# q and k of a head pair in one 128-partition tile, their transposes as 64-row pairs beside the score bursts, another order of the opening, and filling spread by what is ready

## The chip, the cores and the metric

The kernel runs on one core of one Trainium2 chip. The metric is device time in microseconds of one execution, lower is better. The engines named below are PE (TensorE matmul; PEld is its weight load), DVE (VectorE), ACT (ScalarE), POOL (GpSimd) and SP (SyncE, which here only issues DMAs).

## The reference

Block-causal attention, whose output is the input of a maxout feed-forward layer:

```python
# q, k, v: (8 batches, 8 heads, 576 tokens, 64) float32
scores = scale * np.matmul(q, k.transpose(0, 1, 3, 2))
mask = (pos[:, None] // 64) >= (pos[None, :] // 64)
attn = softmax(np.where(mask, scores, -1e9))
x = np.matmul(attn, v).transpose(0, 2, 1, 3).reshape(4608, 512)
g = np.maximum(x @ w1, x @ w2)          # w1, w2: (512, 1024)
out = g @ w_out                         # w_out: (1024, 512)
```

## The kernel before

The work goes by head pairs: 8 batches of 4 pairs, p = 0 to 31. The scheduler is switched off, so each engine executes its instructions in the order in which the code writes them, and waits on semaphores where data or a buffer isn't ready.

For one pair p the steps are these. `load_qk` brings q and k (float32) by two DMAs from SP's queue, each with 8 tokens per partition on 72 partitions. `cast_qk` makes bfloat16 of them, on POOL in the steady state. `transposes(p)` does 16 PE transposes (8 of q into `ps_qT`, 8 of k into `ps_kT`), which DVE copies to `qT` and ACT to `kT`. `burst_a` and `burst_b` are the score matmuls: two heads share each step, head 0 on rows 0 to 63 of the PE array and head 1 on rows 64 to 127. They write four PSUM tiles, here u0 and u1 (`burst_a`) and u2 and u3 (`burst_b`), from a pool `ps_s` of two. `exp` on ACT turns each into `aT`, and memsets (`mask`) on POOL clear the lower half of each diagonal block of 128, two after u0 and u1, two after u2. `av(p, [0, 1])` and `av(p, [2, 3, 4])` multiply with v, whose extra column of ones gives the row sums; DVE makes the reciprocal `rec` and the product `xp`. `x_out` transposes `xp` on PE into `ps_x`, and DVE copies that to `xT`.

The feed-forward matmuls are single steps of 512 columns, which a generator gives out: `h_unit` (8 steps, two PSUM tiles, ended by a DVE copy `h` and a DVE maximum into `g`) and `y_unit` (8 steps, ended by an ACT copy and a DMA of the result). `fill(n)` puts up to n of them between the attention steps on PE. A span of 512 tokens may start once `x_out` of the last pair of a batch has raised `done_tokens`. Before, `fill` asks for 11, 5 and 11 steps in each pair and stops when the generator has none. There are 864 steps in all: 64 belong to the first span and 96 to each further one. One span is released by each of the batches 0 to 6 and two by the last batch, and 224 steps are left after pair 31.

All of the PSUM tiles of transposes, av, x_out, h and y share one pool, `ps_m`, of four banks. v, w1, w2 and w_out come by DMAs that POOL issues (they cast on the way), in the same instruction stream as POOL's casts and memsets. In the opening, v's first DMA stands ahead of the memsets that DVE does on the v tiles; w1 and w2 are issued within pair 0, v of batch 1 and w_out within pair 1.

Of the kernel before, what the change touches and what calls it, by code (L numbers as in the profile page):

```python
# [14 lines left out]
def kernel(  # L15
# [68 lines left out]
    def load_qk(p):  # L84
        b, hp = divmod(p, HP)
        raws[p] = []
        for nm, src in (("q", q), ("k", k)):
            t = raw.tile([P, 2, RPP * D], FP32, name=f"{nm}raw")
# [4 lines left out]
            raws[p].append(t)  # L93

    def cast_qk(p, engines):
        qk_n[p] = []
        for nm, t, copy in zip("qk", raws.pop(p), engines):
            n = qkn.tile([P, RPP, 2, D], BF16, name=f"{nm}n")
            copy(  # L99
                out=n[:NP].rearrange("p t h d -> p h t d"),  # L100
                in_=t[:NP].rearrange("p h (t d) -> p h t d", d=D),
            )
            qk_n[p].append(n)
# [89 lines left out]
    def moe():  # L193
        ny = SPAN // P
        for i in range(NSPAN):
            for f in range(NFF):
                while done_tokens[0] < (i + 1) * SPAN:
                    yield False
                for _ in h_unit(i, f):
                    yield True  # L200
# [17 lines left out]
    def transposes(p):  # L218
        b, hp = divmod(p, HP)
        tiles = []  # L220
        for nm, src in zip("qk", qk_n.pop(p)):
            pt = ps_m.tile([P, RPP, NP], BF16, name=f"ps_{nm}T", tag="m")
            for j in range(RPP):
                nc.tensor.transpose(  # L224
                    pt[:, j, :], src[:NP, j].rearrange("p h d -> p (h d)"), ident[:NP, :NP],
                )
            t = (qT_r if nm == "q" else kT_r)[p % NT]
            dst = t[:, :S].rearrange("q (p j) -> q p j", j=RPP)
            sv = pt.rearrange("q j p -> q p j")
            if nm == "q":  # L230
                nc.vector.tensor_copy(out=dst, in_=sv)
            else:
                nc.scalar.copy(out=dst, in_=sv)  # L233
# [16 lines left out]

    def mask(p, a0, n=1, step=0):
        a = aT_r[p % NA]
        if n == 1:
            nc.gpsimd.memset(a[BLK:, :, a0:a0 + BLK], 0.0)  # L254
        else:
            nc.gpsimd.memset(
                a[BLK:, :, a0:a0 + n * step].rearrange("p h (n s) -> p h n s", s=step)[:, :, :, :BLK],
                0.0,
            )

# [11 lines left out]
    def burst_b(p):  # L272
        u2 = ps_s.tile([P, 2, 512], FP32, name="ps_s", tag="s")
        scores(p, u2, 0, 2, 256, 320)
        scores(p, u2, 320, 3, 384, 192)
# [3 lines left out]
        nc.gpsimd.memset(aT_r[p % NA][BLK:, :, 1024:1088], 0.0)  # L279
        nc.gpsimd.memset(aT_r[p % NA][BLK:, :, 1344:1408], 0.0)  # L280
# [41 lines left out]
    for p in range(NPAIR):  # L322
        b, hp = divmod(p, HP)
        burst_a(p)
        fill(11)
        burst_b(p)
        if p + 3 < NPAIR:
            load_qk(p + 3)
        if p + 2 < NPAIR:
# [45 lines left out]
```

## Time and profile before

| | before |
|---|---|
| median of 3 runs | 343.23 us (341.82 to 343.73) |
| profiled execution | 338.89 us, span 337.1 us |
| PE busy | 292.4 us (87%) |
| PE weight loads busy | 157.5 us (47%) |
| DVE busy | 178.5 us (53%) |
| ACT busy | 138.8 us (41%) |
| POOL busy | 125.4 us (37%) |

The span is the time from the first to the last instruction of the profiled execution; the device time holds 1.8 us more. A busy share is an average over stages that differ: here an opening without feed-forward steps, the stage in which attention and filling run together, and a tail of feed-forward steps alone.

### The profile page before, as it was taken

What the parts mean: (1) busy time and instruction counts of PE and PEld (TensorE: products, weight loads), DVE (VectorE), ACT (ScalarE), POOL (GpSimd) and SP (SyncE); (2) the same over time, 40 slices, a digit from 0 to 9 for tenths busy, and PEclk for the clock granted to TensorE, in tenths of its full rate; (3) what the DMA queues carried; (4) which work ended last, traced back from release to release, by engine and by line L of the source; (5) the groups of instructions that cost most, each with busy time, mean ns of one, the idle gap of its engine ahead of it and who ended that gap; (6) DMA issues with size and microseconds to landing.
All of it is one profiled execution on the core that took longest, in us unless ns stands there. A gap on an engine that the chain in (4) does not pass through costs nothing.

```text
span 337.1 us, 7097 instructions
## 1 busy us (share of the span) xinstructions
PE 292.4 (87%) x2880; PEld 157.5 (47%) x2880; DVE 178.5 (53%) x353; ACT 138.8 (41%) x198; POOL 125.4 (37%) x244
## 2 busy tenths in 40 slices
PE   0065469996999999999999999999999998999995
PEld 0053245554555545555555555555555554444442
DVE  0242124775556655665666566656656665455440
ACT  2053434436545454545454545454554444101112
POOL 2329643554554345434543554355433300000000
PEclk9999999999999999999999999999999999999999
DMA  7899997674087559754875478548853000011013
GB/s 144 168 163 185 222 163 173 92 98 26 2 134 110 124 131 135 112 119 133 129 117 120 118 126 121 123 126 111 132 118 98 31 33 34 31 62 64 31 62 124
DMA packets 57984, 36.63 MB, mean 109 GB/s; under 512 B 39008, under 2 KB 44128, under 8 KB 57952
## 3 DMA queue, kind: packets, MB, share of 16 engines
q0 software_dynamic: 42784, 7.87, 31.5%
q1 hardware_dynamic: 15168, 28.32, 29.0%
q8 instruction: 22, 0.36, 0.5%
q14 instruction: 10, 0.08, 0.1%
HBM read 34.60 MB, written 9.44 MB: 131 GB/s over the span
## 4 chain that ended last, share of the span: by engine, by line
PE 80%; DMA 7%; issue 4%; DVE 3%; ACT 2%; POOL 2%; POOLq 0%; ACTq 0%
PE ps_h L165 37%; PE ps_y L183 18%; PE ps_o L295 10%; PE ps_s L241 7%; DMA w_sb<-in_moe_w_dram 4%; DMA vv<-in_v_dram 4%; PE ps_x L314 3%; PE ps_qT L224 2%; PE ps_kT L224 2%; ACT aT L247 2%; DVE xp L303 2%; POOL w_sb L118 1%; DVE rec L301 1%; DVE vv L130 0%; POOL qn L99 0%
## 5 line engine op out<-in xcount | busy, mean ns | idle before, releaser
L247 ACT ACTIVATE aT<-ps_s 128x1024 bf16<-128x1024 f32 (+1 forms) x128 | 99.2, 831 | 120.1 <-PE ps_s L241 119.1
L165 PE MATMUL ps_h<-xT,w_sb 128*128 128x512 bf16 x576 | 139.2, 381 | 0.0
L165 PEld LDWEIGHTS <-w_sb 128*128 128x128 bf16 x576 | 52.3, 98 | 60.7 <-issue 6.2
L172 DVE CAST h<-ps_h 128x512 bf16<-128x512 f32 x72 | 49.6, 689 | 43.9 <-PE ps_h L165 43.5
L183 PE MATMUL ps_y<-wo_sb,g 128*128 128x512 bf16 x288 | 70.6, 379 | 0.0
L174 DVE TENSOR_TENSOR g<-h,ps_h 128x512 bf16<-128x512 bf16 x72 | 49.5, 687 | 13.3 <-PE ps_h L165 12.1
L295 PE MATMUL ps_o<-vv,aT 128*128 128x65 bf16 x960 | 43.6, 200 | 7.8 <-POOL aT L254 6.9
L301 DVE RECIPROCAL rec<-ps_o 128x4 f32<-128x4 f32 x64 | 12.1, 190 | 66.8 <-PE ps_o L295 66.7
L295 PEld LDWEIGHTS <-aT 128*128 128x128 bf16 x960 | 37.8, 102 | 18.9 <-POOL aT L254 7.2
L254 POOL MEMSET aT<- 64x128 bf16 x64 | 12.7, 200 | 85.4 <-ACT aT L247 85.3
L241 PE MATMUL ps_s<-qT,kT 64*128 64x64 bf16 (+4 forms) x384 | 37.0, 296 | 6.2 <-ACT aT L247 5.5
L183 PEld LDWEIGHTS <-g 128*128 128x128 bf16 x288 | 26.9, 98 | 31.1 <-issue 1.3
L189 ACT COPY y<-ps_y 128x512 f32<-128x512 f32 x36 | 21.2, 588 | 48.0 <-PE ps_y L183 42.2
L108 POOL DMA_DIRECT2D vv<-in_v_dram x40 | 33.8, 852 | 11.8 <-DVE vv L129 11.0
L303 DVE TENSOR_TENSOR xp<-ps_o,rec 128x256 bf16<-128x256 f32 x64 | 31.4, 491 | 2.2
L99 POOL CAST qn<-qraw 72x1024 bf16<-72x1024 f32 x30 | 31.2, 1039 | 1.9
L99 POOL CAST kn<-kraw 72x1024 bf16<-72x1024 f32 x30 | 31.3, 1043 | 0.0
L224 PE MATMUL ps_qT<-ident,qn 72*128 72x72 bf16 x256 | 14.8, 205 | 18.0 <-DVE qn L99 18.0
L233 ACT COPY kT<-ps_kT 128x576 bf16<-128x576 bf16 x32 | 20.1, 628 | 22.0 <-PE ps_kT L224 21.9
L241 PEld LDWEIGHTS <-kT 64*128 64x128 bf16 x384 | 14.8, 97 | 30.6 <-issue 22.3
L279 POOL MEMSET aT<- 64x128 bf16 x32 | 6.4, 201 | 55.0 <-ACT aT L247 55.0
L314 PE MATMUL ps_x<-ident,xp 128*128 128x128 bf16 x160 | 17.4, 230 | 8.8 <-DVE xp L303 8.8
(24 smaller groups left out, 109.5 us busy)
## 6 DMA issues: line engine op xcount, KB each, us to landing
qraw<-in_q_dram SPq DMA_DIRECT2D x32, 288.0 KB
kraw<-in_k_dram SPq DMA_DIRECT2D x32, 288.0 KB
out_dram<-y SPq DMA_DIRECT2D x36, 256.0 KB
vv<-in_v_dram POOLq DMA_DIRECT2D x32, 128.0 KB, 5.8
w_sb<-in_moe_w_dram POOLq DMA_DIRECT2D x8, 256.0 KB, 8.1
wo_sb<-in_moe_w_out_dram POOLq DMA_DIRECT2D x2, 512.0 KB, 13.0
vv<-in_v_dram POOLq DMA_DIRECT2D x8, 64.0 KB, 3.3
```

Of the source, the lines that this page charges most:

```text
L99: copy(out=n[:NP].rearrange("p t h d -> p h t d"), in_=t[:NP].rearrange("p h (t d) -> p h t d", d=D),)
L108: nc.gpsimd.dma_start(out=vv[:rows, c, :, :D], in_=v[b, :, c * P:c * P + rows, :].rearrange("h p d -> p h d"),)
L165: nc.tensor.matmul(pt[:], w_sb[:, c, f * P:(f + 1) * P], xT[:, c, t0:t0 + SPAN], start=(c == 0), stop=(c == NDM - 1),)
L172: nc.vector.tensor_copy(out=h1[:], in_=pt[:])
L174: nc.vector.tensor_max(g[:, f, :], h1[:], pt[:])
L183: nc.tensor.matmul(py[:], g[:, f, s * P:(s + 1) * P], wo_sb[:, f, :], start=(f == 0), stop=(f == NFF - 1),)
L224: nc.tensor.transpose(pt[:, j, :], src[:NP, j].rearrange("p h d -> p (h d)"), ident[:NP, :NP],)
L241: nc.tensor.matmul(ps[:m, hh, col:col + w], kT[r, c * P:c * P + m], qT[r, q0:q0 + w], start=True, stop=True,)
L247: nc.scalar.activation(out=aT_r[p % NA][:m, :, a0:a0 + w], in_=ps[:m, :, :w], func=AF.Exp, scale=scale,)
L295: nc.tensor.matmul(po[:, gi, hh, :], a[:, hh, a0:a0 + P], vv[:, c, 2 * hp + hh, :], start=(mm == 0), stop=(mm == n_mm - 1),)
L303: nc.vector.tensor_mul(xp[:, :n], po[:, :, :, :D], rec[:, :n].to_broadcast([P, n, 2, D]))
L314: nc.tensor.transpose(pt[:, t, :], src.rearrange("p a d -> p (a d)"), ident[:])
```

## The change

Six things change. (1) q and k of a pair lie in one tile of 128 partitions, q on 0 to 63 and k on 64 to 127, 9 tokens per partition; one cast does both. (2) `transposes` does 18 transposes of 64 columns, q and k in turn, on the two row halves of the array; they stand between `fill` and `burst_b` instead of behind `av(p, [0, 1])`. (3) `x_out` does 9 transposes of 64 rows into two PSUM tiles with two DVE copies, and stands at the head of the next pair. (4) In the opening the memsets stand ahead of v's DMAs; all weights, v of batch 1 and w_out are issued from POOL before pair 0; for the first pairs DVE does the masks and the copy of kT. q and k are loaded four pairs ahead (three before). (5) The steps that are ready (`ready`) are divided over the pairs of the batch: 16 per pair in batch 1, 24 in batches 2 to 6, split 2/5, 1/5, 2/5; 27 in the last batch. (6) `xT` is 64 columns longer, so that the copy of five blocks fits.

```diff
-    RPP = 8
-    NP = S // RPP
+    NP = 64
+    RPP = S // NP
...
+        raws[p] = t = raw.tile([P, 2, RPP * D], FP32, name="raw")
+        for r, src in ((0, q), (NP, k)):
             nc.sync.dma_start(
-                out=t[:NP],
+                out=t[r:r + NP],
...
-    for p in range(3):
-        load_qk(p)
-    load_v(0, 0)
+    load_qk(0)
     make_identity(nc, ident)
...
-    cast_qk(0, (nc.vector.tensor_copy, nc.scalar.copy))
-    for c in range(1, NCH):
+    for p in range(1, 4):
+        load_qk(p)
+    for c in range(NCH):
         load_v(0, c)
-    cast_qk(1, (nc.vector.tensor_copy, nc.vector.tensor_copy))
+    cast_qk(0, dve)
+    cast_qk(1, pool)
+    load_w(0, 256)
+    cast_qk(2, pool)
+    load_w(256, 256)
+    load_w(512, 256)
+    cast_qk(3, pool)
+    load_w(768, 256)
+    for c in range(NCH):
+        load_v(1, c)
+    load_wo(0, 4)
+    load_wo(4, 4)
...
+    def ready():
+        n = at[0]
+        while n < len(needs) and needs[n] <= done_tokens[0]:
+            n += 1
+        return n - at[0]
 
     def fill(n):
-        for _ in range(n):
-            if not next(moe_steps, False):
-                return
+        for _ in range(min(n, ready())):
+            next(moe_steps)
+            at[0] += 1
...
+        for j in range(RPP):
+            for r, pt in ((0, pq), (NP, pk)):
+                nc.tensor.transpose(
+                    pt[:, j, :], n[r:r + NP, j].rearrange("p h d -> p (h d)"),
+                    ident[r:r + NP, r:r + NP],
+                )
...
+        for pt, ring_, copy in ((pq, qT_r, dve), (pk, kT_r, dve if p < HP else act)):
...
+        eng = nc.vector if p < HP else nc.gpsimd
+        eng.memset(aT_r[p % NA][BLK:, :, a0:a0 + BLK], 0.0)
...
-            nc.tensor.transpose(pt[:, t, :], src.rearrange("p a d -> p (a d)"), ident[:])
-        px = pt.rearrange("p t w -> p (t w)")[:, :S]
-        nc.vector.tensor_copy(out=xT[:, hp, b * S:(b + 1) * S], in_=px)
+            nc.tensor.transpose(pe[:, t, :], src[:BLK], ident[:BLK, :BLK])
+            if t < NCH - 1:
+                nc.tensor.transpose(po[:, t, :], src[BLK:], ident[BLK:, BLK:])
...
+        nc.vector.tensor_copy(out=dst[:, :, 0], in_=pe[:])
+        nc.vector.tensor_copy(out=dst[:, :NCH - 1, 1], in_=po[:])
...
+        if p > 0:
+            x_out(p - 1)
         burst_a(p)
-        fill(11)
-        burst_b(p)
-        if p + 3 < NPAIR:
-            load_qk(p + 3)
-        if p + 2 < NPAIR:
-            cast_qk(p + 2, (nc.gpsimd.tensor_copy, nc.gpsimd.tensor_copy))
...
-        av(p, [0, 1])
+        n = -(-ready() // (HP - hp)) if p < NPAIR - HP else 27
+        fill(n * 2 // 5)
         if p + 1 < NPAIR:
             transposes(p + 1)
-        fill(5)
+        burst_b(p)
...
+        av(p, [0, 1])
+        fill(n // 5)
         av(p, [2, 3, 4])
-        fill(11)
-        x_out(p)
-    while next(moe_steps, None) is not None:
-        pass
+        fill(n - n * 2 // 5 - n // 5)
+    x_out(NPAIR - 1)
+    fill(len(needs))
```

Two places of the engines' order show what the diff does not. The first is ACT in the steady state, two pairs with feed-forward steps between them (`aT<-ps_s` is an exp, `kT<-ps_kT` the copy of the next pair's transposed k, `y<-ps_y` a result tile). Before:

```order
47 L247 ACTIVATE aT_97<-ps_s 64x2x64
48 L233 COPY kT_93<-ps_kT 128x576
49 L189 COPY y<-ps_y 128x512
50 L247 ACTIVATE aT_98<-ps_s 128x2x512 x3
51 L247 ACTIVATE aT_98<-ps_s 64x2x64
52 L233 COPY kT_92<-ps_kT 128x576
```

and in the changed kernel:

```order
47 L185 COPY y<-ps_y 128x512
48 L252 ACTIVATE aT_97<-ps_s 128x2x512 x2
49 L235 COPY kT_93<-ps_kT 128x576
50 L252 ACTIVATE aT_97<-ps_s 128x2x512
51 L252 ACTIVATE aT_97<-ps_s 64x2x64
52 L185 COPY y<-ps_y 128x512
```

The copy of kT stood behind the four exps of a pair; now it stands between the exps of u1 and u2.

The second place is POOL's opening, from its first DMA to the masks of the first pair that it serves (`vv` is v, `w_sb` is w1 and w2, `wo_sb` w_out, `aT` the masks). Before:

```order
6 L108 DMA vv_94<-in_v_dram 128x8x64
10 L108 DMA vv_94<-in_v_dram 128x8x64 x3
11 L108 DMA vv_94<-in_v_dram 64x8x64
12 L254 MEMSET aT_97 64x2x64 x2
13 L279 MEMSET aT_97 64x2x64
14 L280 MEMSET aT_97 64x2x64
15 L99 CAST qn<-qraw 72x2x8x64
16 L99 CAST kn<-kraw 72x2x8x64
17 L118 DMA w_sb<-in_moe_w_dram 128x4x256 x8
18 L254 MEMSET aT_98 64x2x64 x2
```

and in the changed kernel:

```order
9 L103 DMA vv_94<-in_v_dram 128x8x64 x4
10 L103 DMA vv_94<-in_v_dram 64x8x64
11 L96 CAST qkn<-raw 128x1152
12 L114 DMA w_sb<-in_moe_w_dram 128x4x256 x2
13 L96 CAST qkn<-raw 128x1152
14 L114 DMA w_sb<-in_moe_w_dram 128x4x256 x4
15 L96 CAST qkn<-raw 128x1152
16 L114 DMA w_sb<-in_moe_w_dram 128x4x256 x2
17 L103 DMA vv_95<-in_v_dram 128x8x64 x4
18 L103 DMA vv_95<-in_v_dram 64x8x64
19 L117 DMA wo_sb<-in_moe_w_out_dram 128x4x512 x2
20 L96 CAST qkn<-raw 128x1152 x2
```

No mask stands between the loads any more; the casts of pairs 4 and 5 (the last row) stand behind all of them.

## Rows read from the trace of the kernel before

**Rows 1.** Busy time by stretch: width, then PE, PEld, DVE, ACT, POOL, clock, DMA share, GB/s.

```profile
19.90:26.80 6.90, 5.24 (x63) 3.68 (x63) 2.02 (x5) 3.64 (x5) 3.67 (x8) 1.00 0.77 184
...
54.70:86.00 31.30, 27.64 (x317) 15.06 (x316) 20.34 (x40) 14.60 (x20) 14.95 (x29) 1.00 0.60 78
86.00:251.80 165.80, 161.94 (x1744) 87.81 (x1744) 101.41 (x200) 83.51 (x120) 75.87 (x146) 1.00 0.64 118
251.80:284.80 33.00, 32.03 (x334) 17.18 (x334) 19.62 (x39) 16.18 (x23) 7.05 (x21) 1.00 0.18 56
284.80:337.10 52.30, 48.43 (x225) 21.72 (x222) 22.54 (x33) 7.04 (x12) 0.00 (x0) 1.00 0.16 60
```

**Rows 2.** Timeline of the opening: start, us, instruction, and what ended the idle time.

```profile
6.18 1.04 ACT L99 CAST kn<-kraw 72x1024 bf16<-72x1024 f32 x1 [4.15 <-DMA kraw<-in_k_dram]
13.44 0.09 DVE L129 MEMSET vv<- 128x40 bf16 x1 [13.44 <-DMA vv<-in_v_dram]
...
17.35 1.22 DVE L99 CAST qn<-qraw 72x1024 bf16<-72x1024 f32 x2
...
18.03 0.66 PE L224 MATMUL ps_qT<-ident,qn 72*128 72x72 bf16 x8 [18.03 <-DVE qn L99]
...
18.49 0.68 PE L224 MATMUL ps_kT<-ident,kn 72*128 72x72 bf16 x8
19.09 0.75 DVE L231 COPY qT<-ps_qT 128x576 bf16<-128x576 bf16 x1
...
19.90 1.03 PE L241 MATMUL ps_s<-qT,kT 64*128 64x512 bf16 x6 [0.73 <-ACT kT L233]
```

**Rows 3.** Busy time by stretch, of three short ones in the opening.

```profile
12.00:15.00 3.00, 0.00 (x0) 0.00 (x0) 1.04 (x4) 0.00 (x0) 1.17 (x2) 1.00 0.76 195
15.50:18.00 2.50, 0.00 (x0) 0.00 (x0) 2.02 (x11) 0.00 (x0) 1.67 (x3) 1.00 1.68 107
...
31.00:36.00 5.00, 3.23 (x51) 2.98 (x51) 2.03 (x5) 0.64 (x1) 4.90 (x10) 1.00 1.43 191
```

**Rows 4.** The chain that ended last, one piece: start, us, what.

```profile
29.53 11.99 DMA w_sb<-in_moe_w_dram
```

**Rows 5.** Timeline of PE in one full pair with 27 feed-forward steps.

```profile
158.17 2.54 PE L165 MATMUL ps_h<-xT,w_sb 128*128 128x512 bf16 x11
160.55 0.44 PE L314 MATMUL ps_x<-ident,xp 128*128 128x128 bf16 x5
160.93 0.61 PE L241 MATMUL ps_s<-qT,kT 64*128 64x512 bf16 x6
161.47 1.25 PE L165 MATMUL ps_h<-xT,w_sb 128*128 128x512 bf16 x5
...
163.94 0.42 PE L241 MATMUL ps_s<-qT,kT 64*128 64x320 bf16 x6
164.30 0.35 PE L295 MATMUL ps_o<-vv,aT 128*128 128x65 bf16 x6
164.49 0.43 PE L224 MATMUL ps_qT<-ident,qn 72*128 72x72 bf16 x8
...
165.01 0.60 PE L183 MATMUL ps_y<-wo_sb,g 128*128 128x512 bf16 x2
...
166.19 0.88 PE L295 MATMUL ps_o<-vv,aT 128*128 128x65 bf16 x24
166.91 0.59 PE L165 MATMUL ps_h<-xT,w_sb 128*128 128x512 bf16 x2
```

**Rows 6.** Timeline of ACT in the same pair.

```profile
164.44 1.18 ACT L247 ACTIVATE aT<-ps_s 128x1024 bf16<-128x1024 f32 x2 [1.08 <-PE ps_s L241]
165.52 0.63 ACT L233 COPY kT<-ps_kT 128x576 bf16<-128x576 bf16 x1
```

**Rows 7.** Timeline of PE in pair 6, where no steps were left.

```profile
76.50 0.42 PE L241 MATMUL ps_s<-qT,kT 64*128 64x320 bf16 x6
...
78.34 0.83 PE L295 MATMUL ps_o<-vv,aT 128*128 128x65 bf16 x22 [0.54 <-POOL aT L279]
```

More of the change, by code (lines that the diff above doesn't have):

```diff
@@ L85, in load_qk, with cast_qk @@
         b, hp = divmod(p, HP)
-        raws[p] = []
-        for nm, src in (("q", q), ("k", k)):
-            t = raw.tile([P, 2, RPP * D], FP32, name=f"{nm}raw")
+        raws[p] = t = raw.tile([P, 2, RPP * D], FP32, name="raw")
+        for r, src in ((0, q), (NP, k)):
             nc.sync.dma_start(
-                out=t[:NP],
+                out=t[r:r + NP],
                 in_=src[b, 2 * hp:2 * hp + 2].rearrange("h (p t) d -> p h (t d)", t=RPP),
             )
[L93 to L103, printed above, removed]
+    def cast_qk(p, copy):
+        t = raws.pop(p)
+        qk_n[p] = n = qkn.tile([P, RPP, 2, D], BF16, name="qkn")
+        copy(
+            out=n.rearrange("p t h d -> p t h d"),
+            in_=t.rearrange("p h (t d) -> p t h d", d=D),
+        )
     def load_v(b, c):
-        vv = vv_r[b % NV]
         rows = min(P, S - c * P)
         nc.gpsimd.dma_start(
-            out=vv[:rows, c, :, :D],
+            out=vv_r[b % NV][:rows, c, :, :D],
             in_=v[b, :, c * P:c * P + rows, :].rearrange("h p d -> p h d"),
@@ L115, with load_w @@
     wor = moe_w_out.rearrange("(c p) f -> p c f", p=P)
-    def load_w(dst, src, f0, fw):
-        nc.gpsimd.dma_start(out=dst[:, :, f0:f0 + fw], in_=src[:, :, f0:f0 + fw])
+    def load_w(f0, fw):
+        for dst, src in ((w1_sb, w1r), (w2_sb, w2r)):
+            nc.gpsimd.dma_start(out=dst[:, :, f0:f0 + fw], in_=src[:, :, f0:f0 + fw])
     def load_wo(c0, n):
         nc.gpsimd.dma_start(out=wo_sb[:, c0:c0 + n, :], in_=wor[:, c0:c0 + n, :])
-    for p in range(3):
-        load_qk(p)
-    load_v(0, 0)
+    dve, pool, act = nc.vector.tensor_copy, nc.gpsimd.tensor_copy, nc.scalar.copy
+    load_qk(0)
     make_identity(nc, ident)
@@ L195, in moe @@
         for i in range(NSPAN):
+            need = (i + 1) * SPAN
             for f in range(NFF):
[L197 to L200, printed above, removed]
+                yield from ((need, 0) for _ in h_unit(i, f))
                 if i > 0 and f % 2 == 0:
-                    for _ in y_unit(i - 1, f // 2):
-                        yield True
+                    yield from ((need, 0) for _ in y_unit(i - 1, f // 2))
@@ L204, in moe @@
         for s in range(ny):
-            for _ in y_unit(NSPAN - 1, s):
-                yield True
-    moe_steps = moe()
+            yield from ((NTOK, 0) for _ in y_unit(NSPAN - 1, s))
+    needs = []
+    for i in range(NSPAN):
+        needs += [(i + 1) * SPAN] * (2 * NDM * NFF + (SPAN // P * NFF if i else 0))
+    needs += [NTOK] * (SPAN // P * NFF)
+    moe_steps = moe()
+    at = [0]
+    def ready():
[3 more added lines that the diff above has]
+        return n - at[0]
@@ L210, in fill @@
     def fill(n):
-        for _ in range(n):
-            if not next(moe_steps, False):
-                return
+        for _ in range(min(n, ready())):
+            next(moe_steps)
+            at[0] += 1
     st = {}
     def transposes(p):
-        b, hp = divmod(p, HP)
-        tiles = []
[L221 to L233, printed above, removed]
+        n = qk_n.pop(p)
@@ new lines, in transposes @@
+        pq = ps_m.tile([P, RPP, NP], BF16, name="ps_qT", tag="m")
+        pk = ps_m.tile([P, RPP, NP], BF16, name="ps_kT", tag="m")
+        for j in range(RPP):
[3 more added lines that the diff above has]
+                    ident[r:r + NP, r:r + NP],
+                )
+        tiles = []
+        for pt, ring_, copy in ((pq, qT_r, dve), (pk, kT_r, dve if p < HP else act)):
+            t = ring_[p % NT]
+            copy(
+                out=t[:, :S].rearrange("q (p j) -> q p j", j=RPP),
+                in_=pt.rearrange("q j p -> q p j"),
+            )
@@ L249, in exp, with mask @@
         )
[L251 to L259, printed above, removed]
+    def mask(p, a0):
+        eng = nc.vector if p < HP else nc.gpsimd
+        eng.memset(aT_r[p % NA][BLK:, :, a0:a0 + BLK], 0.0)
     def burst_a(p):
@@ L278, in burst_b @@
         exp(p, u2, 512, 1024)
[L279 to L280 removed]
+        mask(p, 1024)
+        mask(p, 1344)
         exp(p, u3, 64, 1536, m=BLK)
```

29 lines of the change are left out of this document (12 added, 17 removed).

## The prediction

> **What bounds the kernel now.** I read the busy time by stretch first, then the timelines of the opening and of one pair, then the chain that ended last. The stretches [rows 1] show four regimes. Up to 54.7 us PE does attention alone: a pair costs 6.9 us where nothing disturbs it, and PE is busy for 5.24 of these. From 54.7 to 86.0 the pairs 4 to 7 share 64 feed-forward steps. From 86.0 to 251.8 twenty pairs share 480 steps, with PE busy for 161.94 of 165.8 us: PE is the bound there, and a PE microsecond saved counts only if no other engine's chain takes it back. The last batch costs 33.0 us, and the tail, 224 steps, 52.3 us, of which the change touches nothing. A step costs 48.43 / 225 = 0.215 us.
>
> The opening is bounded by order, not by work [rows 2]. k of pair 0 has landed by 6.18, but DVE starts its memsets at 13.44 only, because v's first DMA was issued ahead of them and they wait for its landing; so the first transposes begin at 18.03 and the first scores at 19.90. Further on the chain holds a wait of 11.99 us for a weight DMA [rows 4], with POOL's masks queued behind it: a pair that needed 6.9 us then takes 11.5.
>
> **The change, part by part.** All terms are made against the profiled execution (338.89 us, span 337.1); the median of the three runs lies 4.3 us above it, which I add at the end.
>
> *First scores.* The memsets move ahead of v's DMAs and are done before q and k land. One cast of 1152 elements replaces those of 1024: 0.61 x 1152 / 1024 = 0.69 us [rows 2], so 6.2 to 6.9. The transposes run there at about half rate (eight in 18.49 - 18.03 = 0.46 us, against 16 in 0.52 later [rows 2, 5]); the clock column reads 1.00 in all stretches, so I take the spacing itself. With their landing that ends near 7.7. Both copies of 0.75 us now stand on DVE: 9.2. First scores at 9.3 instead of 19.9.
>
> *Pairs 0 to 3.* All loads are issued at once, so the DMAs must be added up. q and k alone move 195 GB/s with the DMA engines at share 0.76, v alone 107, weights alone 191 [rows 3]. In SBUF bytes a pair's q and k are 0.59 MB (3.0 us), v of a batch 0.59 MB (5.5 us), w1 and w2 2.1 MB (11 us). Pair 0 needs all of v's first batch before its second av. v and the first four pairs' q and k together take 17.6 us from 1.5: 19.1 if everything must land, 14 if v gets its share early (then exps and masks decide). I take 17, and 18.5 for the first scores of pair 1. Pairs 1 to 3 take 6.9 us each, plus 0.1 for the kT copy that DVE now does between masks: pair 4 starts at 39.5 instead of 54.7. Weights, v of batch 1 and q and k of pairs 4 to 7 are another 28.6 us, so the last of v lands at 47.7 if all else goes ahead of it, and near 43 if the queues share; pair 4's second av stands at about 43.5, so I count no wait. By the Trainium skill (DMA: Bandwidth & Descriptors, on why a DMA increments its semaphore by 16) a load issued from SP is spread over the largest number up to 16 of engines that divides its outer size: 12 for 72 partitions, 16 for 64. The share of 0.76 agrees with 12 of 16; by that rule q and k would take 2.2 us a pair, and the bound of 47.7 would be 41.
>
> *PE in a full pair.* The old q and k transposes take 165.01 - 164.49 = 0.52 us, x_out 160.93 - 160.55 = 0.38, of which a change of the array's row mode is about 0.10: the 11 steps from 161.47 end at 163.84, and the next scores, on half the rows, start at 163.94 [rows 5]. There are four such changes per pair now (x_out to scores, scores to fill, fill to scores, scores to av), and four afterwards (fill to x_out, scores to fill, fill to transposes, scores to av). So standing beside the bursts saves no change of mode; what is saved is the streaming. Score matmuls of the two halves run side by side: 1024 columns for each of two heads from 160.93 to 161.47, in 0.44 us without the change of mode, 2.3 columns per ns and half. If the new transposes do the same, 9 x 64 columns take 0.25 us and x_out's 5 x 64 take 0.14: 0.27 + 0.14 = 0.41 saved. If they run one behind the other, the nearest row is av, 24 matmuls of 65 columns in 0.72: 0.030 each, 0.54 + 0.27, and nothing is saved. I take side by side, since the score rows are the same half-array form.
>
> *The wait that takes its place.* The kT copy (0.63 us [rows 6]) used to stand behind the pair's exps; now it stands between those of u1 and u2, and av of tiles 2 to 4 is queued behind exp u2 and its masks. How long that chain is, a pair without steps shows: scores at 76.50, av's third matmul at 78.34, after a wait for the mask: 1.84 us [rows 7]. There exp u2 begins 0.50 after the scores (163.94 to 164.44 [rows 5, 6]). Now the copy can begin when the last transpose has landed, about 0.27 after the scores' start, and frees ACT at 0.79 (0.63 less the 0.1 by which ACT's instructions overlap): exp u2 is 0.29 late, and the third av matmul can't start before 2.13. PE gets there by itself after scores (0.36), first av (0.19), four steps (0.86) and two matmuls (0.06): 1.47. Before, five steps and the transposes stood there, so the mask was never late, only 0.10 of a bank wait (166.19 against 165.01 + 5 x 0.215). So 0.66 us of idle PE replace 0.10. Bounds: 0.37 if the copy cost ACT nothing, 1.0 if the whole copy counted.
>
> *The sum per pair.* A full pair now takes 166.91 - 158.17 = 8.74 for 27 steps, so 2.92 without them; afterwards 2.92 - 0.41 - 0.10 + 0.66 = 3.07. With 24 steps that is 8.23, and 0.2 more once per batch, where the first steps wait for two DVE copies behind g's. Twenty pairs: 165.6 against 165.8, since the old mean of 8.29 contains the starved fourth pair of each batch. **The saving on PE and the even filling are given back to ACT's chain; this stretch stays as it is.** Pairs 4 to 7 with 16 steps: 3.45 + 3.07 = 6.5, 0.1 more for one step less in the middle, and 2 us for the first steps at half rate: 28.4 instead of 31.3. The last batch: three pairs with 27 steps at 8.65 and a last without transposes of 6.8: 32.7. The tail stays at 52.3, with 0.4 for the xT copies.
>
> POOL casts once per pair instead of twice and loses nothing; DVE's second xT copy stands where DVE waits (busy 101.41 of 165.8 [rows 1]).
>
> Span: 39.5 + 28.4 = 67.9 for the start of pair 8 (86.0 before), + 165.6 + 32.7 + 52.7 = 318.9; 18.2 less than 337.1. From the median: 343.2 - 18.2 = 325.0.
>
> **The rivals.** (A) *The pairs of transposes don't run side by side:* 0.41 us in 28 pairs, 11.5 us: 336.5. For it: every new transpose brings its own weight load, and no row shows half-array loads in a dense row. A rule of the Trainium skill speaks for it (TensorE: Matmul & The Clock Gate, on 56 and 53 ns): starts never come closer than 25 ns, however small the matmul. By it 27 transposes would take 0.68 instead of 0.39, 8 us in all; the score pairs, which stand in for them here, contradict it at 0.44 us for six. (B) *ACT's chain costs less*, half of 0.66: 9 us less, 316. Against: the wait of rows 7 is of this very form. (C) *The opening is bound by DMA and POOL:* POOL's w_out issue waits for older DMAs, as in rows 4, and the cast of pair 4 stands behind it; if v and that cast come 8 us late, 333. (D) *Slower:* each half-array transpose pays for an unhidden weight load. The change loses when that costs more than the 18 us, 0.65 per pair, so from 0.039 us for each of the 27 one behind the other; at the 0.058 of the opening's transposes [rows 2] it is 1.18 per pair, 33 us: 358.
>
> **How the numbers follow.** Forecast 0.50, A 0.17, C 0.15, B 0.10, D 0.04, A and C at once (344.5) 0.04. The range goes from 314 (just short of B, with the opening's good end) to 337 (A and C in it), leaving out about 0.18. Half a per cent, 1.7 us, is about what can be told from no change. Faster: 0.92; same, A and C cancelling it: 0.03; slower, D and the worse half of A and C: 0.05.
>
> **What would show it.** First scores near 9 us; pair 4 near 40; 18 transposes in 0.25 to 0.3 us; an idle gap of some 0.6 us on PE inside each second av, released by POOL's mask; ACT's kT copy in front of the third exp; the middle twenty pairs again at 8.2 to 8.3 us. I am wrong if that gap is absent (faster than 316), if the 18 take 0.5 us, or if pair 8 starts after 75 us.

## The result: 331.62 us, 3.1% faster, and the profile after

The changed kernel takes 331.62 us (median of 4 runs, 331.25 to 332.61), the kernel before 342.52 beside it (4 runs, 340.61 to 343.73): a ratio of 0.969, 95% interval 0.964 to 0.974. The forecast was 325.0. The profiled spans are 330.8 and 337.1 us: 6.3 apart, less than the medians (10.9), because the profiled run of before lies 3.6 us under its median and that of the changed kernel 1.0 us above its own. Of 28 further executions of the kernel before, the six with a mean granted clock of 1.00 took 337.61 to 340.58 us (like the profiled one) and the 22 with 0.985 to 0.989 took 341.57 to 345.84, while all four of the changed kernel had 0.999 or 1.000, so by the median of those six (339.7) about 3 of the 10.9 us are probably the clock (an estimate), and no kept trace shows where before loses it. The stages below are compared by spans.

Busy time by stretch of the changed kernel, with the columns of [rows 1]; the stretches are pair 0, pairs 1 to 3, pairs 4 to 7, the middle twenty pairs, the last four, and the tail:

```profile
10.36:29.60 19.24, 4.72 (x68) 3.08 (x70) 3.19 (x10) 3.12 (x4) 9.53 (x12) 1.00 1.33 203
29.60:50.10 20.50, 14.04 (x211) 10.05 (x213) 10.47 (x35) 9.53 (x13) 7.72 (x9) 1.00 1.55 210
50.10:79.20 29.10, 26.44 (x342) 13.75 (x344) 19.51 (x43) 14.61 (x20) 11.60 (x25) 1.00 0.78 100
79.20:245.50 166.30, 155.54 (x1866) 79.99 (x1868) 102.44 (x220) 84.77 (x120) 57.95 (x125) 1.00 0.66 117
245.50:278.30 32.80, 31.07 (x363) 15.96 (x361) 20.69 (x44) 16.09 (x23) 5.27 (x18) 1.00 0.10 39
278.30:330.80 52.50, 48.61 (x229) 21.87 (x227) 22.57 (x34) 7.02 (x12) 0.00 (x0) 1.00 0.16 61
```

By spans all that was gained stands ahead of pair 8, which starts at 79.2 instead of 86.0. The middle takes 166.3 us against 165.8, although PE is busy for 6.4 us less in it (155.54 against 161.94 [rows 1]): what PE saved, it now waits. And pair 0 alone takes 19.24 us, with PE busy for 4.72.

The timeline of the opening shows why (start, us, instruction, and what ended the idle time ahead of it):

```profile
1.44 4.34 POOL L103 DMA_DIRECT2D vv<-in_v_dram  x5
...
6.77 1.35 DVE L96 CAST qkn<-raw 128x1152 bf16<-128x1152 f32 x1 [1.82 <-DMA raw<-in_k_dram]
8.15 0.59 SPq L88 DMA_DIRECT2D raw<-in_q_dram  x1
...
10.36 1.04 PE L246 MATMUL ps_s<-qT,kT 64*128 64x512 bf16 x6 [1.52 <-DVE kT L235]
...
15.38 0.44 PE L294 MATMUL ps_o<-vv,aT 128*128 128x65 bf16 x5 [1.28 <-DMA vv<-in_v_dram]
...
15.72 0.60 SPq L88 DMA_DIRECT2D raw<-in_q_dram  x1
...
23.51 0.54 PE L294 MATMUL ps_o<-vv,aT 128*128 128x65 bf16 x7 [7.70 <-DMA vv<-in_v_dram]
...
27.65 0.98 PE L294 MATMUL ps_o<-vv,aT 128*128 128x65 bf16 x15 [3.60 <-DMA vv<-in_v_dram]
```

v's five DMAs are issued by 5.8, but PE waits 1.28, 7.70 and 3.60 us for their landings. Between issue and landing SP issues q and k of pairs 4, 5 and 6 (8.15, 12.64, 15.72), each as soon as a cast has freed one of the four `raw` buffers.

A steady pair of the middle, PE, then ACT, then POOL:

```profile
156.69 0.20 PE L228 MATMUL ps_qT<-ident,qkn 64*128 64x64 bf16 x1
156.69 0.20 PE L228 MATMUL ps_kT<-ident,qkn 64*128 64x64 bf16 x1
156.72 0.19 PE L228 MATMUL ps_qT<-ident,qkn 64*128 64x64 bf16 x1
...
156.96 0.41 PE L246 MATMUL ps_s<-qT,kT 64*128 64x320 bf16 x6
157.31 0.34 PE L294 MATMUL ps_o<-vv,aT 128*128 128x65 bf16 x6
157.49 1.03 PE L179 MATMUL ps_y<-wo_sb,g 128*128 128x512 bf16 x4
158.36 0.22 PE L294 MATMUL ps_o<-vv,aT 128*128 128x65 bf16 x2
159.12 0.83 PE L294 MATMUL ps_o<-vv,aT 128*128 128x65 bf16 x22 [0.54 <-POOL aT L258]
159.79 0.81 PE L179 MATMUL ps_y<-wo_sb,g 128*128 128x512 bf16 x3
```

```profile
157.24 0.64 ACT L235 COPY kT<-ps_kT 128x576 bf16<-128x576 bf16 x1 [0.71 <-PE ps_kT L228]
157.78 1.18 ACT L252 ACTIVATE aT<-ps_s 128x1024 bf16<-128x1024 f32 x2
```

```profile
158.87 0.35 POOL L258 MEMSET aT<- 64x128 bf16 x2 [2.08 <-ACT aT L252]
```

A q and a k transpose start together, the next two 0.03 later; the 18 take 156.96 - 156.69 = 0.27 us, where 16 took 0.52 [rows 5]. The five and four transposes of `x_out` in the same pair take 154.08 - 153.95 = 0.13 us, up to the next scores. Then the second av has its gap: 159.79 - 158.36 = 1.43 us for 24 matmuls that take 0.72 undisturbed [rows 5], so 0.71 idle. The chain back is mask, exp u2, kT copy: exp u2 stood ready when the scores had landed, but begins at 157.78, behind the copy.

### The profile page after: what moved, and what is told of

The parts are those of the page before. It is cut to its first block, busy times and chain, and to the rows that moved or that the text cites. A ratio compares the mean times of both kernels' runs of the same rounds, so it can differ in the third digit from the quotient of the medians.

```text
span 330.8 us, 7470 instructions
## 1 busy us (share of the span) xinstructions
PE 281.1 (85%) x3072; PEld 145.2 (44%) x3072; DVE 184.4 (56%) x403; ACT 136.4 (41%) x193; POOL 97.1 (29%) x199
## 3 DMA queue, kind: packets, MB, share of 16 engines
q1 hardware_dynamic: 14400, 28.32, 32.8%
## 4 chain that ended last, share of the span: by engine, by line
PE 48%; issue 26%; ACT 11%; DMA 7%; POOL 5%; DVE 2%; POOLq 0%; ACTq 0%; DVEq 0%
PE ps_h L161 24%; PE ps_y L179 11%; ACT aT L252 10%; PE ps_o L294 8%; DMA vv<-in_v_dram 7%; POOL aT L258 3%; PE ps_s L246 3%; PE ps_xe L314 2%; POOL vv L103 1%; DVE xp L302 1%; DVE qT L235 0%; DVE kT L235 0%; POOL qkn L96 0%; ACT y L185 0%; DVE rec L300 0%
## 5 line engine op out<-in xcount | busy, mean ns | idle before, releaser
L179 PE MATMUL ps_y<-wo_sb,g 128*128 128x512 bf16 x288 | 74.7, 379 | 0.0
L294 PE MATMUL ps_o<-vv,aT 128*128 128x65 bf16 x960 | 47.9, 200 | 29.9 <-POOL aT L258 14.4
L258 POOL MEMSET aT<- 64x128 bf16 x112 | 20.8, 199 | 157.9 <-ACT aT L252 146.8
L294 PEld LDWEIGHTS <-aT 128*128 128x128 bf16 x960 | 39.2, 101 | 43.8 <-POOL aT L258 17.7
L300 DVE RECIPROCAL rec<-ps_o 128x4 f32<-128x4 f32 x64 | 11.8, 185 | 56.0 <-PE ps_o L294 55.9
L96 POOL CAST qkn<-raw 128x1152 bf16<-128x1152 f32 x31 | 35.5, 1147 | 8.0 <-DMA raw<-in_k_dram 6.2
L235 DVE COPY qT<-ps_qT 128x576 bf16<-128x576 bf16 x32 | 24.1, 752 | 4.4 <-PE ps_kT L228 3.2
L235 ACT COPY kT<-ps_kT 128x576 bf16<-128x576 bf16 x28 | 17.9, 639 | 17.6 <-PE ps_kT L228 17.3
L228 PE MATMUL ps_qT<-ident,qkn 64*128 64x64 bf16 x288 | 15.3, 200 | 9.5 <-DVE qkn L96 8.2
L246 PEld LDWEIGHTS <-kT 64*128 64x128 bf16 x384 | 17.7, 99 | 10.1 <-issue 4.2
L228 PEld LDWEIGHTS <-qkn 64*128 64x128 bf16 x576 | 12.0, 101 | 22.3 <-DVE qkn L96 8.2
L228 PE MATMUL ps_kT<-ident,qkn 64*128 64x64 bf16 x288 | 15.3, 200 | 0.0
```

The lines of the kernel that those rows point to most:

```text
L96: copy(out=n.rearrange("p t h d -> p t h d"), in_=t.rearrange("p h (t d) -> p t h d", d=D),)
L179: nc.tensor.matmul(py[:], g[:, f, s * P:(s + 1) * P], wo_sb[:, f, :], start=(f == 0), stop=(f == NFF - 1),)
L228: nc.tensor.transpose(pt[:, j, :], n[r:r + NP, j].rearrange("p h d -> p (h d)"), ident[r:r + NP, r:r + NP],)
L235: copy(out=t[:, :S].rearrange("q (p j) -> q p j", j=RPP), in_=pt.rearrange("q j p -> q p j"),)
L246: nc.tensor.matmul(ps[:m, hh, col:col + w], kT[r, c * P:c * P + m], qT[r, q0:q0 + w], start=True, stop=True,)
L294: nc.tensor.matmul(po[:, gi, hh, :], a[:, hh, a0:a0 + P], vv[:, c, 2 * hp + hh, :], start=(mm == 0), stop=(mm == n_mm - 1),)
```

## Experiments

Each edit is against the changed kernel unless the text names another base. Times are medians of 4 runs; "middle" is the mean of pairs 8 to 27 in the profiled run (8.31 us in the changed kernel).

### Opening: is it the early loads that hold v up?

Two `raw` buffers instead of four, and each load written behind the cast that frees its buffer:

```diff
-    raw = ctx.enter_context(tc.tile_pool(name="raw", bufs=4))
+    raw = ctx.enter_context(tc.tile_pool(name="raw", bufs=2))
...
-    for p in range(1, 4):
-        load_qk(p)
+    load_qk(1)
     for c in range(NCH):
         load_v(0, c)
     cast_qk(0, dve)
+    load_qk(2)
     cast_qk(1, pool)
+    load_qk(3)
...
-        if p + 4 < NPAIR:
-            load_qk(p + 4)
         if 4 <= p + 2 < NPAIR:
             cast_qk(p + 2, pool)
+        if p + 4 < NPAIR:
+            load_qk(p + 4)
```

> Two buffers for raw q and k instead of four, the rest as changed; q and k of pairs 2 to 5 can then be loaded only as the casts free a buffer. Theory (q and k of pairs 4 to 6, loaded too early, hold up v of batch 0): the last of v lands near 20 us instead of 28, the first scores of pair 1 stand near 21 instead of 29.6, and the time falls by 6 to 8 us, to about 324.5. Rival (v's small packets or the weights behind them are slow in themselves): v still lands at 26 to 28 us and the time stays within 1.5 us. If the loads then come too late for pairs 2 to 4, part of the gain is lost there.

Measured: 322.99 us (321.70 to 323.75), 8.6 less. PE's first wait in an av of pair 0 is now for a mask, none is for v:

```profile
15.78 1.39 PE L295 MATMUL ps_o<-vv,aT 128*128 128x65 bf16 x22 [0.70 <-DVE aT L259]
...
36.26 0.23 PE L229 MATMUL ps_qT<-ident,qkn 64*128 64x64 bf16 x1 [3.22 <-POOL qkn L96]
```

Pair 1 starts at 18.2 (forecast 18.5) and pair 8 at 69.7 (forecast 67.9); the last of v lands at 15.2 us instead of 27.65. So the early loads of later pairs were the cause, and v's packets are not slow in themselves. The edit holds back pairs 2 and 3 too (issued at 7.76 and 13.36 instead of 3.48 and 5.12), so how much of the 11 us belongs to pairs 4 to 6 alone isn't separated. The second row is the next thing that is late, and it stands behind POOL's DMA issues, as rival C had it: the transposes of pair 4 wait 3.22 us for POOL's cast. On POOL that cast stands behind the issues of v of batch 1 and of w_out, one of which waits 2.79 us for a weight DMA:

```profile
31.87 0.69 POOL L103 DMA_DIRECT2D vv<-in_v_dram  x1 [2.79 <-DMA w_sb<-in_moe_w_dram]
...
35.05 2.24 POOL L96 CAST qkn<-raw 128x1152 bf16<-128x1152 f32 x2
```

### Middle: what sets the gap in the second av?

Three edits, each on the changed kernel. First, seven steps instead of four between the two av groups, and seven instead of nine ahead of the transposes:

```diff
-        fill(n * 2 // 5)
+        fill(n * 3 // 10)
...
-        fill(n // 5)
+        fill(n * 3 // 10)
...
-        fill(n - n * 2 // 5 - n // 5)
+        fill(n - 2 * (n * 3 // 10))
```

> The steps of a pair split 3/10, 3/10, 4/10 instead of 2/5, 1/5, 2/5: with 24 steps 7, 7, 10 instead of 9, 4, 11. Theory (PE idles 0.7 us inside the second av for a mask that is late because the kT copy stands ahead of the third exp): three more steps there take 0.65 us, the gap goes, the twenty middle pairs take 7.65 us instead of 8.31, the time falls by 14 to 18 us. Rival (the gap only moves: two steps less ahead of the transposes leave PE waiting for the exps of u0 and u1): less than 4 us.

Measured: 319.82 us (319.58 to 319.99), middle 7.82: 11.8 us less, short of the 14 to 18 expected. The second av takes its 0.72 us again, but the first step behind av now waits for a PSUM bank of `ps_m` that the kT copy empties:

```profile
151.05 0.35 PE L294 MATMUL ps_o<-vv,aT 128*128 128x65 bf16 x6
151.68 1.46 PE L179 MATMUL ps_y<-wo_sb,g 128*128 128x512 bf16 x6 [0.28 <-ACT kT L235]
```

Second, the transposes (still row pairs) back in their old place, behind `av(p, [0, 1])`:

```diff
-        if p + 1 < NPAIR:
-            transposes(p + 1)
         burst_b(p)
...
         av(p, [0, 1])
+        if p + 1 < NPAIR:
+            transposes(p + 1)
```

> The row-pair transposes put back behind the first av, ahead of the middle steps, the rest as changed; the array's row mode then changes six times a pair instead of four (0.2 us more). Theory (the kT copy ahead of the third exp makes the mask late): the copy stands behind the exps again, the gap inside the second av falls from 0.7 us to under 0.15, the middle pairs take 7.8 us instead of 8.31, the time falls by 10 to 15 us. Rival (the gap comes from the shorter middle alone): the gap stays above 0.4 us and the time within 5 us.

Measured: 320.14 us (319.37 to 320.40), middle 7.81, as expected. The kT copy again stands behind the exps (ACT):

```profile
158.40 1.18 ACT L252 ACTIVATE aT<-ps_s 128x1024 bf16<-128x1024 f32 x2 [0.65 <-PE ps_s L246]
159.47 0.63 ACT L235 COPY kT<-ps_kT 128x576 bf16<-128x576 bf16 x1
```

No wait for a mask shows on PE in the second av of that pair. It goes from 159.79 to the step at 160.72, 0.93 us, 0.21 more than undisturbed, where the changed kernel loses 0.71.

Third, only the engine of the kT copy:

```diff
-        for pt, ring_, copy in ((pq, qT_r, dve), (pk, kT_r, dve if p < HP else act)):
+        for pt, ring_, copy in ((pq, qT_r, dve), (pk, kT_r, dve)):
```

> The changed kernel with one edit: DVE copies kT in all pairs, not ACT; the order on PE is untouched. Theory: the gap in the second av (0.72 us) is exp u2 being late behind the kT copy on ACT (0.64 us, 0.5 of it counted). Without it exp u2 starts about 0.25 us earlier, when the scores have landed, and the gap falls to about 0.4: middle pair 8.0, total near 325. Rival: the gap is set by exps u0 and u1 and the masks on POOL alone, or DVE's longer queue makes rec and xp late: middle pair stays at 8.3 or grows.

Measured: 323.17 us (323.00 to 323.17), middle 7.99: the gap falls from 0.71 to 0.39 (the second av goes from 161.25 to the step at 162.36), with PE's order as it was:

```profile
161.69 0.83 PE L294 MATMUL ps_o<-vv,aT 128*128 128x65 bf16 x22 [0.21 <-POOL aT L258]
```

The kT copy on ACT is 0.32 of it; the rest is the chain of exp u2 and its mask against only four steps.

### Do the transposes need to be written in turn?

All q transposes, then all k ones, and the same for x_out's halves:

```diff
-        for j in range(RPP):
-            for r, pt in ((0, pq), (NP, pk)):
+        for r, pt in ((0, pq), (NP, pk)):
+            for j in range(RPP):
```

> The same transposes, all of q first and then all of k, and in x_out all even blocks and then all odd ones: half-array as before, no two of different halves in turn. Theory (the two halves run side by side only when they stand in turn): 18 transposes take 0.54 us instead of 0.27 and x_out 0.26 instead of 0.13, the middle pairs take 8.7 us instead of 8.31, the time rises by 8 to 12 us. Rival (the order within the group does not matter, or another wait hides it): within 2 us.

Measured: 336.09 us (335.34 to 336.51), middle 8.46: 4.5 us slower instead of 8 to 12, and 0.15 a pair instead of 0.4. The halves overlap although they are not written side by side. On PE:

```profile
158.17 0.35 PE L228 MATMUL ps_qT<-ident,qkn 64*128 64x64 bf16 x6
158.34 0.20 PE L228 MATMUL ps_kT<-ident,qkn 64*128 64x64 bf16 x1
158.35 0.19 PE L228 MATMUL ps_qT<-ident,qkn 64*128 64x64 bf16 x1
...
158.50 0.31 PE L246 MATMUL ps_s<-qT,kT 64*128 64x320 bf16 x1
158.52 0.25 PE L228 MATMUL ps_kT<-ident,qkn 64*128 64x64 bf16 x3
```

The first k transpose starts at 158.34, while three q transposes that are written ahead of it start later, and the first score matmul begins ahead of the last three k transposes.

### Both losses taken away, and what is then late

Two raw buffers and the old place of the transposes together (the first and the third diff above):

> The two edits that gained most on different sides, together: two raw buffers (so that the loads of pairs 4 to 6 don't stand beside v of batch 0) and the transposes behind av of tiles 0 and 1 (so that ACT's copy of kT stands behind the exps). If the two losses are independent, the gains add up: 331.6 - 8.6 - 11.5 = 311.5, with pair 8 at about 68 and 7.81 us a middle pair. Rival: the losses share something (POOL's masks being late when pairs come earlier, weights landing late against an earlier pair 4): then pair 8 stays near 69.7 but pairs 4 to 7 or the middle wait more, 314 to 318.

Measured: 310.91 us (310.00 to 311.62), pair 8 at 67.8, middle 7.81. The gains add up, 331.62 - 8.63 - 11.48 = 311.51, so the two losses are independent. The next three are built on this one.

POOL's issue of v of batch 1 and w_out moved behind its casts of pairs 4 and 5:

```diff
-    for c in range(NCH):
-        load_v(1, c)
-    load_wo(0, 4)
-    load_wo(4, 4)
...
             cast_qk(p + 2, pool)
+        if p == 2:
+            for c in range(NCH):
+                load_v(1, c)
+        if p == 3:
+            load_wo(0, 4)
+            load_wo(4, 4)
```

> As the first of these, with v of batch 1 issued within pair 2 and w_out within pair 3, behind POOL's casts of pairs 4 and 5, so that those casts don't stand behind DMA issues which wait for older weights. Theory: with two raw buffers pair 4 came 9.2 us after pair 3 instead of 6.9 because of those casts; now 6.9, pair 4 near 39 and pair 8 near 66, total 309.5. Rival: v of batch 1 now lands later than pair 4's first av needs it (issued near 32, beside weights), and what is gained at pair 4 is lost there: total unchanged.

Measured: 311.59 us (310.01 to 312.55), no gain. Pair 4 starts at 36.4 instead of 39.2, but takes 11.8 us instead of 8.6, and the chain says for what:

```profile
30.96 13.79 DMA vv<-in_v_dram
...
44.79 1.13 PE ps_o L291 x15
```

This is the rival of that expectation: the cast no longer waits, v of batch 1 does. But v is only half of the 3.2 us: PE waits for it 1.09 and 0.45 us in the second av, and then runs at a lower clock. Over pair 4 the granted clock is 0.86:

```profile
36.40:48.20 11.80, 9.85 (x89) 4.47 (x91) 4.54 (x11) 3.64 (x5) 3.78 (x8) 0.86 1.78 191
```

It is 0.50 from 44.0 to 45.7, behind 1.5 us in which PE was busy for 0.41, and the last seven steps of the pair take 2.35 us, against 1.61 in the base kernel.

### What are the row pairs worth?

q and k in two tiles of 72 partitions again, with two casts and 16 transposes, all else as in the kernel of 310.91 us:

```diff
-    NP = 64
-    RPP = S // NP
+    RPP = 8
+    NP = S // RPP
...
-        for j in range(RPP):
-            for r, pt in ((0, pq), (NP, pk)):
+        for n, pt in zip(nn, (pq, pk)):
+            for j in range(RPP):
                 nc.tensor.transpose(
-                    pt[:, j, :], n[r:r + NP, j].rearrange("p h d -> p (h d)"),
-                    ident[r:r + NP, r:r + NP],
+                    pt[:, j, :], n[:NP, j].rearrange("p h d -> p (h d)"), ident[:NP, :NP],
                 )
```

> The kernel with two raw buffers and the transposes behind av of tiles 0 and 1 (310.9 us), with q and k in two tiles of 72 partitions again: two casts and 16 transposes of 72 rows, q then k, as before the change; all else stays. The prediction's theory: the row pairs save streaming (0.52 us against 0.27), so a middle pair takes 0.25 us more and the total is near 319. Rival: in this place, between av and the steps, which both use all rows, the row pairs bring two changes of the array's row mode, which transposes of 72 rows don't need there (0.37 us from the transposes' start to the step against 0.52, but 0.28 from av to the transposes against 0.19): then only 0.06 a pair, total 311 to 314. The opening should also be later where q and k move with 12 of 16 DMA engines busy.

Measured: 314.98 us (314.84 to 315.44), middle 7.86: 0.05 us a pair, the rival's case, not the 0.25 of the prediction's theory. (Another 3 us are lost in pair 0, where v is late again by 6.68 us; SP's loads of pairs 2 and 3 are issued earlier there, from 5.66 to 10.18 instead of 7.63 to 13.68. The first scores are not later, as expected, but earlier, 8.02 instead of 9.84: the casts of pair 0 begin at 4.88 and 5.76 instead of 6.25 and are shorter.) PE, first with two tiles of 72 rows, then with the row pairs:

```profile
144.12 0.42 PE L250 MATMUL ps_s<-qT,kT 64*128 64x320 bf16 x6
144.47 0.35 PE L298 MATMUL ps_o<-vv,aT 128*128 128x65 bf16 x6
144.66 0.43 PE L233 MATMUL ps_qT<-ident,qn 72*128 72x72 bf16 x8
...
145.18 1.03 PE L184 MATMUL ps_y<-wo_sb,g 128*128 128x512 bf16 x4
```

```profile
141.05 0.36 PE L295 MATMUL ps_o<-vv,aT 128*128 128x65 bf16 x6
...
141.71 1.04 PE L180 MATMUL ps_y<-wo_sb,g 128*128 128x512 bf16 x4
```

From av to the next step: 0.71 us and 0.66. The likely reason is the one of the rival, two changes of the row mode between av and the steps, which use all rows: from av to the transposes it is 0.29 us (141.34 - 141.05) with the row pairs and 0.19 (144.66 - 144.47) without. Beside the scores there are no such changes: in the changed kernel scores, transposes and av fill 157.49 - 156.69 = 0.80 us, where with 72 rows they take 145.18 - 144.12 = 1.06. Layout and place earn 0.26 together and the layout alone 0.05; transposes of 72 rows beside the scores were not tried, so what the place alone earns is not shown.

x_out as before the change (five transposes of 128 rows, one copy), same base:

> The same base with x_out as before the change: five transposes of 128 rows into one PSUM tile and one DVE copy, still at the head of the next pair. Prediction's theory: streaming of 0.28 us instead of 0.13, the number of mode changes the same (one between x_out and the scores instead of one between the steps and x_out): 0.14 a pair, total 310.9 + 4.5 = 315.4, middle pair 7.95. Rival: the mode change hides differently, or the second DVE copy and PSUM bank cost what the row pairs save: total 311.

Measured: 315.14 us (314.81 to 315.22), middle 7.95, 0.14 a pair: the term of the prediction's sum. What the second DVE copy and PSUM bank cost is in it and not separated.

### The even filling

```diff
-        n = -(-ready() // (HP - hp)) if p < NPAIR - HP else 27
+        n = 27
```

> The changed kernel with one edit: each pair asks for 27 steps, as before, and takes what is ready (27, 27, 27, 15 in batches 2 to 6) instead of an even 24. Theory of the prediction: PE's time per pair is 3.07 us plus 0.215 a step plus the gap, and the gap shrinks by a step's time where five steps instead of four stand ahead of it: three pairs of four have 0.2 less, the fourth pair (10 and 5 steps and nothing at its end) has its gap too and an x_out that waits for DVE (0.3 to 0.5). Middle pair 8.2 to 8.3, total 329 to 332: even filling is worth nothing here. Rival: the even filling carries the gain of the stretch, since a pair starved of steps waits for ACT (6.9 us of attention alone): then the middle pair is 8.5 or more and the total 336 or more.

Measured: 338.37 us (337.95 to 338.96), 6.8 slower: the expectation fell. But not in the steady batches, which take 33.32 us against 33.26. Batch 1 loses 3.3 us, and pair 8 takes 11.37 instead of 8.32. Busy time by stretch there (the last column but two is the granted clock): the end of pair 7, which has no steps left, and pair 8:

```profile
78.50:81.60 3.10, 1.30 (x34) 1.02 (x34) 1.36 (x4) 1.00 (x2) 1.49 (x3) 0.79 0.47 85
81.60:84.60 3.00, 3.00 (x16) 1.11 (x15) 0.59 (x3) 1.94 (x2) 0.20 (x1) 0.50 0.01 3
84.60:87.30 2.70, 2.70 (x24) 0.92 (x24) 1.32 (x2) 0.00 (x0) 0.20 (x1) 0.53 0.00 0
87.30:93.00 5.70, 5.38 (x76) 2.91 (x70) 3.40 (x7) 2.30 (x4) 3.19 (x5) 1.00 0.16 42
```

PE is busy for 1.30 of 3.10 us, and then runs at half its clock (0.50, the level of 1.2 GHz) for 5.7 us, busy all the time. All four runs have a mean granted clock of 0.990, those of the changed kernel 0.999 or 1.000. An empty pair doesn't always bring this: in the profiled run of the kernel before, pair 7 (from 80.33) has no steps either, and pair 8 behind it runs at 1.00 and takes 8.65 us:

```profile
80.30:83.00 2.70, 1.22 (x16) 0.59 (x15) 0.46 (x1) 2.18 (x3) 1.24 (x4) 1.00 0.38 24
...
86.00:89.00 3.00, 3.00 (x19) 1.20 (x17) 1.65 (x3) 1.94 (x2) 0.60 (x3) 1.00 0.02 5
```

To tell the clock from something late in pair 8 itself, 27 steps from batch 2 on only (`if p < 2 * HP` in that line):

> The changed kernel with 27 steps asked for from batch 2 on, but batch 1 spread evenly (16 a pair). With 27 in all batches 6.8 us were lost: 3.3 in batch 1 and 3.05 in pair 8, whose steps ran at 0.45 us with a granted clock of 0.50 behind a pair 7 without steps; the later batches cost the same (33.32 a batch against 33.26). Theory: PE fell to its lower clock because pair 7 left it mostly idle, so with pair 7 filled pair 8 takes 8.75 and the total is 331.6 + 0.3 to 0.6, about 332. Rival: pair 8 is slow because 27 steps there need something late (weights of w_out, the PSUM banks of y): 11.4 again, total 334.5 to 335.

Measured: 331.76 us (331.34 to 332.24); pair 8 takes 8.75 with the clock at 1.00:

```profile
72.40:79.20 6.80, 6.09 (x85) 3.33 (x87) 5.03 (x13) 3.54 (x5) 1.89 (x5) 1.00 0.53 97
79.20:88.00 8.80, 8.37 (x96) 4.33 (x98) 5.71 (x14) 4.40 (x7) 3.58 (x7) 1.00 0.20 36
```

So even filling is worth nothing where a batch is full and 6.6 us in batch 1, of which 2.6 (11.37 - 8.75, both with 27 steps) are the clock behind an empty pair.

### A version that beats both

Two raw buffers; the transposes where the change put them; steps split 9, 7, 8; v of batch 1 issued ahead of all weights but the first quarter:

```diff
     cast_qk(2, pool)
-    load_w(256, 256)
-    load_w(512, 256)
-    cast_qk(3, pool)
-    load_w(768, 256)
     for c in range(NCH):
         load_v(1, c)
-    load_wo(0, 4)
-    load_wo(4, 4)
+    cast_qk(3, pool)
+    load_w(256, 256)
...
             cast_qk(p + 2, pool)
+        if p in (2, 3):
+            load_w((p - 2) * 256 + 512, 256)
+        if p in (5, 6):
+            load_wo((p - 5) * 4, 4)
...
-        fill(n // 5)
+        fill(n * 3 // 10)
         av(p, [2, 3, 4])
-        fill(n - n * 2 // 5 - n // 5)
+        fill(n - n * 2 // 5 - n * 3 // 10)
```

> The changed kernel with two raw buffers, the transposes where the change put them, steps split 9, 7 and 8 (instead of 9, 4 and 11), and the opening's POOL queue in another order: v of batch 1 ahead of all weights but the first quarter, the last two quarters and w_out behind the casts of pairs 4 and 5. Theory for the middle: seven steps cover the gap, and the first of them finds its PSUM bank already taken, so the 0.23 us wait of the 7, 7, 10 split is gone: 7.65 to 7.7 us a pair. Theory for the opening: pair 4 at 36.5, no wait for v of batch 1, pair 8 at 65 to 66. Total near 305. Rival: the bank wait only moves (middle 7.8), or the first steps of batch 1 now wait for their weights (pair 8 at 68): 308 to 311.

Measured: 304.76 us (304.61 to 305.16), a ratio of 0.892 (0.883 to 0.901) to the kernel before. Pairs 0 to 3, 4 to 7 and the middle:

```profile
9.80:37.60 27.80, 18.52 (x277) 13.13 (x277) 13.68 (x45) 12.65 (x17) 15.66 (x18) 1.00 1.81 191
37.60:65.90 28.30, 26.85 (x347) 14.05 (x347) 19.58 (x43) 14.61 (x20) 13.14 (x27) 1.00 1.08 165
65.90:219.30 153.40, 153.40 (x1868) 79.85 (x1862) 102.56 (x222) 84.79 (x120) 57.98 (x125) 1.00 0.81 131
```

In the middle PE is busy for 153.40 of 153.40 us, as the rows have it, and a pair takes 7.67; pair 4 starts at 37.6 (36.5 expected). Of the nine steps ahead of the transposes the last is y's first (137.29 in one pair), so y's bank is already taken when the kT copy holds the others; the seven behind them (138.41) begin without a wait and cover exp u2 and its mask. What the order of the opening and the split each earn was not taken apart.

## Why the prediction was right, and where its size was off

The direction and the account of the steady pair held; the size of the opening did not. By the prediction's own sign (wrong "if pair 8 starts after 75 us") the opening was wrong: pair 8 starts at 79.2. That 331.62 comes as near to 325.0 as it does is in part luck: the sum starts from 343.2, in which before probably loses some 3 us to its clock that the changed kernel doesn't lose, and the prediction has no term for that. Rival C's 333 comes closer, although the waits that it names (w_out's issue, the cast of pair 4) are not the ones that made the changed kernel late. By spans 6.3 of the forecast 18.2 us came.

- **First scores:** forecast 9.3, measured 10.36. The cast began 0.57 us later than assumed (6.77, when k had landed) and took 1.35 us for its 1152 elements, not 0.69; one of 1024 on 72 partitions takes 0.69 to 0.76 in the kernel with 72 rows. Whether the partitions or the ninth token make the difference was not tried. The 2.2 us a pair that the prediction names for q and k on 64 partitions is not seen in these rows: with 72 partitions (the kernel of 314.98 us) pair 0 had landed by 5.76, with 128 (that of 310.91) by 6.25.
- **Pairs 0 to 3: the mis-sized term.** "All loads are issued at once" was the step that failed. I counted q and k of the first four pairs beside v, 17.6 us of DMA, and took pair 1 at 18.5. But four raw buffers and a load four pairs ahead let SP issue three more pairs' q and k before v had landed, and v came at 27.65: pair 1 at 29.6, 11.1 us late. By the prediction's own prices seven pairs and v are 7 x 3.0 + 5.5 = 26.5 us from 1.5, so 28.0 (an estimate), near the 27.65. With two buffers pair 1 starts at 18.2; that comes near the 18.5, but behind a mask and with pairs 2 and 3 held back, so it doesn't test the sum. The total miss by spans is 330.8 - 318.9 = 11.9: this term and the first scores, which stand inside it. Where rival C put 8 us on w_out's issue, v of batch 0 cost 11.1. Which of the other edits of the opening (memsets, masks and kT copy on DVE) earn what was not taken apart.
- **Pairs 1 to 7:** 20.5 us for three pairs (21.0 forecast), 29.1 for four (28.4).
- **PE in a full pair:** right. 18 transposes 0.27 us (0.25 forecast, rival A 0.54), x_out 0.13 (0.14). The row that the prediction held against rival A's floor, six score matmuls in 0.44 us, could not test it: six starts 25 ns apart need 0.15. The Trainium skill's floor (TensorE: Matmul & The Clock Gate, on 56 and 53 ns: starts never closer than 25 ns) was weighed for A; here the two halves' starts coincide in the rows (156.69 twice), and within one half they are 0.03 apart, so the trace agrees with it only for each half by itself.
- **The wait that takes its place:** right, 0.71 us against 0.66, with the chain as named: kT copy, exp u2, mask. The engine of the copy alone gave 0.32 of it back; the 0.39 that stayed is close to the lower bound, 0.37.
- **Middle, last batch, tail:** 166.3, 32.8 and 52.5 against 165.6, 32.7 and 52.7. The saving on PE was indeed given back to ACT's chain; four different edits took 0.32 to 0.64 us a pair of it back.
- **Even filling:** the prediction priced it only inside the 28.4 us of pairs 4 to 7 (16 steps each), and the clock behind an empty pair not at all. There it earns 6.6 us against 27 steps a pair, so without it the change would have been worth 1% (0.990, 0.983 to 0.997).

## What to carry to other kernels

Count a load against a deadline together with everything that the free buffers let other queues issue before it lands: a deeper prefetch can make the first tile late. An engine's saving counts only when the chain that runs beside it is covered too: move work to where both the mode of the array and the queue of the engine that empties the result stay undisturbed, and put enough independent work behind it. Where work is spread by what is ready, look at the granted clock behind the stretch that would be left empty, in more than one run.

## What the chip showed that I had not expected

- Transposes of the two row halves overlap even when all of one half's are written first: 0.15 us a pair was lost where running one behind the other would have cost 0.4.
- What a row pair saves hangs on its neighbours: 0.05 us a pair between full-row work, 0.26 for layout and place together beside half-row work. That a change of row mode eats the difference fits the 0.29 and 0.19 us from av to the transposes, and was not tested by itself.
- After a pair without steps (PE busy for 1.30 of 3.10 us) the granted clock was 0.50 and 0.53 for 5.7 us of full work; with that pair filled it stayed at 1.00. In the profiled run of before, an empty pair 7 (busy for 1.22 of 2.70 us) left it at 1.00, so such a pair can bring the lower clock and need not.
- In the opening of the changed kernel the first six feed-forward steps, at 51.15, take 2.74 us, about 0.45 each, while the column of the granted clock reads 1.00 there; why spacing and column differ there stays open.
